# Sliding-window attention on one core: half of one K tile moved from TensorE transposes to VectorE blocks and GpSimd moves, loaded earlier; a 128-column ones tile for the range count

## The chip, the cores and the metric

One core of a Trainium2 chip. The metric is the device time of one execution in microseconds (us); lower is better. Executions over 1.5% slower than the fastest of the same kernel are left out of the means. Medians are quoted. Ratios are the mean time of one kernel's runs over that of the other's in the same rounds, so not quite the ratio of those medians.

Engine names in the profile: PE is TensorE's matmuls, PEld its weight loads, DVE is VectorE, ACT ScalarE, POOL GpSimd, and SP the engine whose queue issues most transfers. The granted clock is the share of the full TensorE clock that the trace records. A pitch is the time from the start of one instruction to the start of the next of its kind. The chain of waits is the chain of work that ended last, followed back from the end of the program.

## The reference

```python
B, Sq, D = 8, 32, 1024;  Hq, Hkv, Dh = 32, 4, 128;  W = 2048      # the last W of 8192 cached rows
q = (x @ wq).reshape(B, Sq, Hq, Dh).transpose(0, 2, 1, 3)
k = repeat(k_cache[:, :, -W:, :], Hq // Hkv);  v = repeat(v_cache[:, :, -W:, :], Hq // Hkv)
p = softmax(einsum("bhqd,bhkd->bhqk", q, k) * Dh ** -0.5)
out = einsum("bhqk,bhkd->bhqd", p, v).transpose(0, 2, 1, 3).reshape(B, Sq, Hq * Dh) @ wo
```

## The kernel before

There are 32 units, one for each batch row and KV head. A unit has four slots. In each slot TensorE makes scores for 512 keys (four matmuls), ScalarE exponentiates them, and TensorE multiplies the slot from two slots ago by V. Query projections, output projections and K transposes are fitted between these as side work. I count slots through the whole program: unit u has slots 4u to 4u+3.

Scores need K transposed. There are three ways to get it, chosen per unit:

- units 0 to 4: TensorE transposes 16 blocks of 128x128, VectorE copies them out of PSUM;
- units 5, 8, 11 and so on: VectorE transposes 32x32 blocks inside each quarter (four instructions), then 16 moves of 32x512 put the quarters in place, 12 on GpSimd and 4 on VectorE in unit 5's case;
- the others: a transposing DMA.

```python
PE_T = (0, 1, 2, 3, 4)
V_T = {5: (2, (5, 6, 8, 10), 10, 17, 12), ...}     # unit: (loaded with unit, slots of blocks, moves from slot, to slot, GpSimd's moves)
...
self.krp = pool("krp", 4)      # K as loaded
self.kbp = pool("kbp", 2)      # K after the block transposes
...
    def kv_pieces(self, ui):
        def blocks(i):
            if i == 0:
                st["kb"] = self.kbp.tile([P, KT, P], BF16, name="kb")
            sl = slice(i * KT // 4, (i + 1) * KT // 4)
            nc.vector.transpose(out=st["kb"][:, sl, :], in_=self.k_raw[ui][:, sl, :])
        def move(k, d):
            ...
            out = self.kT[ui][d * 32:(d + 1) * 32, :, k * 32:(k + 1) * 32]
            in_ = st["kb"][k * 32:(k + 1) * 32, :, d * 32:(d + 1) * 32]
            if d >= V_T[ui][4] // 4:
                nc.vector.tensor_copy(out=out, in_=in_)
            else:
                nc.gpsimd.tensor_scalar(out=out, in0=in_, scalar1=1.0, scalar2=1.0, op0=ALU.mult, op1=ALU.mult)
...
            for c in range(NCH):                                   # one slot
                s_ps = self.ps_s.tile([P, CJ, UQ], FP32, name="s_ps")
                for jj in range(CJ):
                    nc.tensor.matmul(s_ps[:, jj, :], lhsT=self.kT[ui][:, c * CJ + jj, :], rhs=q_u, start=True, stop=True)
                pT = self.ptp.tile([P, CJ, UQ], BF16, name="pT")
                nc.scalar.activation(out=pT[:, :, :], in_=s_ps[:, :, :], func=ACT.Exp, bias=0.0, scale=self.scale)
                ...                                                # P*V of two slots ago
                for k in ((c,) if ui else ...) if nxt else ():
                    nxt[k]()                                       # four TensorE transposes of the next unit's K
                for p in plan[ui * NCH + c]:
                    p()                                            # blocks, moves, projections
```

At the end a matmul with a ones tile of one column counts the softmax sums that lie in range; if one did not, a slower exact path would run.

## Time and profile before

| | before |
|---|---|
| time, median | 186.7 us |
| span of the profiled run | 184.6 us |
| PE busy, share of the span | 98% |
| first scores of unit 5 (slot 20) | 37.41 us |
| GpSimd done with unit 5's K | 37.13 us (28.36 + 8.77) |
| step of the count matmul in the chain | 0.15 us |

The first view is the page of the kernel before: its line of busy times and its line of the chain that ended last.

```profile
PE 180.7 (98%) x2057; PEld 154.0 (83%) x2057; DVE 115.1 (62%) x266; ACT 131.7 (71%) x133; POOL 95.0 (51%) x150
...
PE 93%; DMA 4%; SPq 1%; issue 0%; DVE 0%
```

The kernel is bound by TensorE. Time that another engine takes is free as long as TensorE never waits for it. The windows view shows where that is close. Each line is a stretch of 5 us with the busy time of each engine; the last three columns are the granted clock, the DMA share and the rate.

```profile
core 0: us, PE busy (x) PEld busy (x) DVE busy (x) ACT busy (x) POOL busy (x), PEclk, DMA share, GB/s
25.00:30.00 5.00, 5.00 (x77) 4.81 (x75) 4.87 (x11) 4.63 (x5) 1.52 (x3) 1.00 1.02 399
30.00:35.00 5.00, 5.00 (x68) 4.72 (x66) 4.79 (x11) 4.47 (x5) 4.62 (x7) 1.00 1.17 287
35.00:40.00 5.00, 5.00 (x64) 4.67 (x62) 4.90 (x12) 3.63 (x4) 2.18 (x5) 1.00 1.20 192
40.00:45.00 5.00, 5.00 (x61) 4.63 (x59) 2.97 (x9) 3.53 (x4) 4.62 (x7) 1.00 1.11 372
45.00:50.00 5.00, 5.00 (x63) 4.67 (x62) 2.37 (x8) 3.91 (x4) 4.56 (x8) 1.00 1.13 279
```

The averages of the page (VectorE 62%, GpSimd 51%) say that there is room. This view says that VectorE has none between 25 and 40 us. The timeline of GpSimd alone shows the other engine. Columns: start, time, engine, line, operation, and in brackets the idle time before.

```profile
28.36 8.77 POOL L261 TENSOR_SCALAR kTv<-kb 32x512 bf16<-32x512 bf16 x12 [26.79 <-PE s_ps L468]
39.76 11.78 POOL L261 TENSOR_SCALAR kTv<-kb 32x512 bf16<-32x512 bf16 x16 [2.63 <-PE s_ps L468]
```

GpSimd is idle until 28.36 us and then works through unit 5's 12 moves, 0.73 us each on average. They end at 37.13 us. The timeline of all engines shows when the results are wanted.

```profile
31.30 0.65 DVE L238 COPY kT<-tp 128x1024 bf16<-128x1024 bf16 x1
32.11 0.60 PE L468 MATMUL s_ps<-QT_63,kT 128*128 128x256 bf16 x4
...
35.29 0.71 DVE L251 STREAM_TRANSPOSE kb<-k_raw 128x512 bf16<-128x512 bf16 x1
...
37.41 0.60 PE L468 MATMUL s_ps<-QT_63,kTv 128*128 128x256 bf16 x4
...
39.54 0.65 DVE L410 COPY va_114<-v_sb 128x2048 bf16<-128x2048 bf16 x1
...
40.51 0.62 PE L479 MATMUL o_ps<-va_114,pT 128*128 128x129 bf16 x8
```

Unit 5's scores (37.41) come 0.3 us after GpSimd is done, unit 5's V matmuls (40.51) 0.3 us after VectorE's copy (39.54 + 0.65 = 40.19), and unit 4's first scores (32.11) 0.2 us after the copy that feeds them (31.95). All three are just in time. Last, the chain of waits at the end:

```profile
176.38 0.86 PE op_ps L295 x4
177.25 0.15 PE cnt_ps L533
177.40 4.48 PE op_ps L295 x36
```

### The profile page before, as it was taken

How to read it: one execution, taken by the hardware profiler on the slowest of the kernel's cores; microseconds unless marked ns; L12 is line 12 of the kernel's file. 1: busy time of each engine (PE TensorE's matmuls, PEld its weight loads, DVE VectorE, ACT ScalarE, POOL GpSimd, SP SyncE). 2: the span in 40 equal slices, each digit the busy share in tenths (PEclk: the TensorE clock that was granted, in tenths of full speed). 3: DMA queues.
4: the chain of work that ended last, by engine and by line, in shares of the span. 5: the costliest groups of instructions: out<-in, count | busy, mean ns of one | idle time of the engine just before them, and what ended most of it. 6: DMA issues, size and time to landing. Idle time of an engine off the chain costs nothing.

```text
span 184.6 us, 5057 instructions
## 1 busy us (share of the span) xinstructions
PE 180.7 (98%) x2057; PEld 154.0 (83%) x2057; DVE 115.1 (62%) x266; ACT 131.7 (71%) x133; POOL 95.0 (51%) x150
## 2 busy tenths in 40 slices
PE   8999999999999999999999999999999999999994
PEld 2789999999999999988788899988787888888843
DVE  0119799994586686586468549656754865265363
ACT  2207899787789777787878677887776888888800
POOL 2000007949939959928954990797199379700000
PEclk9999999999999999999999999999999999999999
DMA  5999999999999999999999999999999999993003
GB/s 161 283 390 407 408 396 395 260 182 380 262 355 208 389 250 240 340 321 302 233 396 251 303 378 308 240 249 409 301 301 342 260 275 313 282 269 47 0 30 94
DMA packets 52954, 51.73 MB, mean 280 GB/s; under 512 B 39744, under 2 KB 40256, under 8 KB 52928
## 3 DMA queue, kind: packets, MB, share of 16 engines
q1 hardware_dynamic: 52352, 50.90, 99.0%
q10 hardware_dynamic: 576, 0.49, 0.8%
q8 instruction: 16, 0.26, 0.6%
q14 instruction: 10, 0.08, 0.2%
HBM read 41.42 MB, written 0.52 MB: 227 GB/s over the span
## 4 chain that ended last, share of the span: by engine, by line
PE 93%; DMA 4%; SPq 1%; issue 0%; DVE 0%
PE o_ps L479 31%; PE s_ps L468 30%; PE op_ps L295 15%; PE q_ps L275 11%; DMA wq_sb<-in_wq_dram 4%; PE q_ps L376 2%; PE tp L236 2%; SPq L164 1%; PE kf_ps L369 1%; SPq L320 0%; DVE o_t L305 0%; PE cnt_ps L533 0%
## 5 line engine op out<-in xcount | busy, mean ns | idle before, releaser
L470 ACT ACTIVATE pT<-s_ps 128x1024 bf16<-128x1024 f32 x128 | 128.8, 1025 | 32.5 <-PE s_ps L468 31.5
L261 POOL TENSOR_SCALAR kTv<-kb 32x512 bf16<-32x512 bf16 x140 | 94.1, 672 | 64.9 <-PE s_ps L468 38.3
L479 PEld LDWEIGHTS <-pT 128*128 128x128 bf16 x1024 | 68.5, 98 | 3.1
L468 PEld LDWEIGHTS <-kT 128*128 128x128 bf16 x368 | 34.8, 98 | 10.3
L295 PE MATMUL op_ps<-wo_sb,OT 128*128 128x512 bf16 (+2 forms) x144 | 36.2, 355 | 0.0
L275 PE MATMUL q_ps<-xT,wq_sb 128*128 128x256 bf16 x192 | 28.2, 273 | 0.0
L479 PE MATMUL o_ps<-va_112,pT 128*128 128x129 bf16 x352 | 27.1, 220 | 0.0
L479 PE MATMUL o_ps<-va_113,pT 128*128 128x129 bf16 x352 | 27.0, 220 | 0.0
L479 PE MATMUL o_ps<-va_114,pT 128*128 128x129 bf16 x320 | 24.7, 220 | 0.0
L251 DVE STREAM_TRANSPOSE kb<-k_raw 128x512 bf16<-128x512 bf16 x36 | 23.8, 685 | 1.2 <-DMA k_raw<-in_k_cache_dram 1.2
L416 DVE RECIPROCAL RL_all<-o_ps 128x2 f32<-128x2 f32 x32 | 5.3, 164 | 25.8 <-PE o_ps L479 25.7
L421 DVE TENSOR_SCALAR o_sb<-o_ps,RL_all 128x128 bf16<-128x128 f32 x64 | 19.5, 347 | 1.1
L468 PEld LDWEIGHTS <-kTv 128*128 128x128 bf16 x144 | 13.9, 98 | 5.1
L275 PEld LDWEIGHTS <-wq_sb 128*128 128x128 bf16 x192 | 17.0, 98 | 1.2
L468 PE MATMUL s_ps<-QT_63,kT 128*128 128x256 bf16 x112 | 16.8, 272 | 0.0
L423 DVE STREAM_TRANSPOSE OT<-o_sb 128x256 bf16<-128x256 bf16 x32 | 14.2, 445 | 1.1
L468 PE MATMUL s_ps<-QT_66,kT 128*128 128x256 bf16 x96 | 14.4, 273 | 0.0
L295 PEld LDWEIGHTS <-OT 128*128 128x128 bf16 x144 | 11.4, 98 | 2.3 <-DVE OT L423 0.2
L468 PE MATMUL s_ps<-QT_65,kT 128*128 128x256 bf16 x80 | 12.0, 273 | 0.0
L468 PE MATMUL s_ps<-QT_64,kT 128*128 128x256 bf16 x80 | 12.0, 272 | 0.0
L302 DVE TENSOR_TENSOR oacc<-op_ps,oacc 128x512 f32<-128x512 f32 x8 | 5.5, 682 | 7.4 <-PE op_ps L295 7.4
L410 DVE COPY va_113<-v_sb 128x2048 bf16<-128x2048 bf16 x11 | 9.8, 888 | 0.0
(44 smaller groups left out, 105.6 us busy)
## 6 DMA issues: line engine op xcount, KB each, us to landing
v_sb<-in_v_cache_dram SPq DMA_DIRECT2D x30, 512.0 KB, 7.6
wo_sb<-in_wo_dram SPq DMA_DIRECT2D x16, 512.0 KB, 6.9
wq_sb<-in_wq_dram SPq DMA_DIRECT2D x13, 512.0 KB, 7.5
k_raw<-in_k_cache_dram SPq DMA_DIRECT2D x13, 512.0 KB, 6.4
wq_sb<-in_wq_dram SPq DMA_DIRECT2D x6, 256.0 KB, 6.5
v_sb<-in_v_cache_dram SPq DMA_DIRECT2D x4, 256.0 KB, 4.9
kT<-in_k_cache_dram SPq DMA_TRANSPOSE x36, 7.3
k_raw<-in_k_cache_dram SPq DMA_DIRECT2D x2, 256.0 KB, 7.6
```

The source lines that it names most:

```text
L251: nc.vector.transpose(out=st["kb"][:, sl, :], in_=self.k_raw[ui][:, sl, :])
L261: nc.gpsimd.tensor_scalar(out=out, in0=in_, scalar1=1.0, scalar2=1.0, op0=ALU.mult, op1=ALU.mult)
L275: nc.tensor.matmul(st["ps"][:, 0:self.NQ], lhsT=self.wq_t[g, i][:, c % (DC // 2), hl * P:(hl + 1) * P], rhs=self.xT[:, c, :], start=(c == ...
L295: nc.tensor.matmul(ps[:, 0:w], lhsT=self.OT[:, gq, c, t * P:(t + 1) * P], rhs=self.wo_t[gq][:, c, n0:n0 + w], start=(k == 0), stop=(k == 7))
L302: nc.vector.tensor_tensor(out=acc, in0=ps[:, 0:w], in1=acc, op=ALU.add)
L410: self.nc.vector.tensor_copy(out=self.va[ui % 3][:, :, 0:self.Dh], in_=self.v_sb[ui][:, :, :])
L416: nc.vector.reciprocal(out=rl[:, ui * QT_N:(ui + 1) * QT_N], in_=o_ps[:, :, Dh])
L421: nc.vector.tensor_scalar(out=o_sb[:, qt, :, :], in0=o_ps[:, qt, 0:Dh].rearrange("p (i c) -> p c i", c=4), scalar1=rl[:, ui * QT_N + qt:ui ...
L423: nc.vector.transpose(out=self.OT[:, g * QT_N:(g + 1) * QT_N, :, b * self.Sq:(b + 1) * self.Sq], in_=o_sb[:, :, :, :])
L468: nc.tensor.matmul(s_ps[:, jj, :], lhsT=self.kT[ui][:, c * CJ + jj, :], rhs=q_u, start=True, stop=True)
L470: nc.scalar.activation(out=pT[:, :, :], in_=s_ps[:, :, :], func=ACT.Exp, bias=0.0, scale=self.scale)
L479: nc.tensor.matmul(o_ps[:, qt, 0:self.VW], lhsT=pT[:, jj, qt * P:(qt + 1) * P], rhs=va[:, j, 0:self.VW], start=(j == 0 and qt == 0), stop= ...
```

## The change

It has three parts. The intent is to take eight of unit 4's sixteen transposes off TensorE, the engine that bounds the kernel, and give them to engines that look half idle; to let the count matmul use the whole array width; and to load one late V tile in one transfer.

```diff
-V_HALVES = 30
+V_HALVES = 31
+KH = 4
+KH_SLOTS = ((6, 7), 7, 12)          # slots of the two blocks; moves spread from slot 7 to 12
...
-        self.ones_c = self.c1.tile([P, 1], BF16, name="ones_c")
+        self.ones_c = self.c1.tile([P, P], BF16, name="ones_c")
...
+        if ui == KH - 2:
+            self.load_k(KH, 1)       # second half of K4 right after K2 and V2; the first half stays where it was
...
-        return [lambda i=i: piece(i) for i in range(4)]
+        return [lambda i=i: piece(i) for i in range(2 if ui == KH else 4)]
+
+    def kh_pieces(self):
+        def blocks(i):
+            if i == 0:
+                st["kb"] = self.kbp.tile([P, KT, P], BF16, name="kb")
+            sl = slice(i * H // 2, (i + 1) * H // 2)
+            nc.vector.transpose(out=st["kb"][:, sl, :], in_=self.k_raw[KH][:, H + sl.start:H + sl.stop, :])
+        def move(k, d):
+            nc.gpsimd.tensor_scalar(out=self.kT[KH][d * 32:(d + 1) * 32, H:, k * 32:(k + 1) * 32],
+                                    in0=st["kb"][k * 32:(k + 1) * 32, 0:H, d * 32:(d + 1) * 32],
+                                    scalar1=1.0, scalar2=1.0, op0=ALU.mult, op1=ALU.mult)
...
+        blocks, moves = self.kh_pieces()
+        for k, p in enumerate(blocks):
+            plan[KH_SLOTS[0][k]].append(p)
+        spread(moves, *KH_SLOTS[1:])
...
-        nc.tensor.matmul(cnt[0:1, 0:2 * ncol], lhsT=self.ones_c[:, :], rhs=self.ok[:, :, :], start=True, stop=True)
+        nc.tensor.matmul(cnt[:, 0:2 * ncol], lhsT=self.ones_c[:, :], rhs=self.ok[:, :, :], start=True, stop=True)
```

More of the change, by code (lines that the diff above doesn't have):

```diff
@@ L186, in load_k @@
             H = KT // 2
+            if ui == KH and part == 1:
+                self.k_raw[ui] = self.krp.tile([P, KT, self.Dh], BF16, name="k_raw")
+            if ui == KH and part == 0:
+                nc.sync.dma_start(out=self.k_raw[ui][:, 0:H, :], in_=src.rearrange("(p j) d -> p j d", j=KT)[:, 0:H, :])
+                return
             if part == 1:
@@ L210, in load_unit @@
             if ui not in V_T:
-                self.load_k(ui, None if ui in PE_T else 0)
+                self.load_k(ui, None if ui in PE_T and ui != KH else 0)
             self.load_v(ui, self.nc.sync)
@@ L238, in piece @@
                 nc.vector.tensor_copy(out=self.kT[ui][:, half * 8:(half + 1) * 8, :], in_=st["tp"][:, :, :])
-        return [lambda i=i: piece(i) for i in range(4)]
+        return [lambda i=i: piece(i) for i in range(2 if ui == KH else 4)]
+    def kh_pieces(self):
+        nc, P, KT = self.nc, self.P, self.KT
+        H, st = KT // 2, {}
+        def blocks(i):
[7 more added lines that the diff above has]
+                                    scalar1=1.0, scalar2=1.0, op0=ALU.mult, op1=ALU.mult)
+        return [lambda i=i: blocks(i) for i in range(2)], [lambda k=k, d=d: move(k, d) for k in range(4) for d in range(4)]
     def kv_pieces(self, ui):
@@ L485, in run @@
                     pv_queue.pop(0)()
-                for k in ((c,) if ui else ((), (), (0, 1), (2, 3))[c]) if nxt else ():
+                for k in ((c,)[:len(nxt) - c] if ui else ((), (), (0, 1), (2, 3))[c]) if nxt else ():
                     nxt[k]()
```

## The prediction

> **What bounds it.** TensorE. The page gives PE 98% busy at a full clock, and the chain of waits is 93% PE; the windows table shows PE busy 5.00 of every 5.00 us from 15 us on. Counting four-matmul score groups as "slots" (four per unit), the timeline has score slot 6 at 20.98, 10 at 25.43, 18 at 34.76 and 20 (unit 5, the first fed by GpSimd) at 37.41 us.
>
> **What the change takes off PE.** Eight K4 transposes (and a 0.65 us VectorE copy). Four transposes cost 0.22 us (slots with them are 1.11 us apart, without 0.89): 0.45 us. The count matmul takes 0.15 us in the chain of waits, though its 128 columns should stream in a quarter of a 512-column matmul's 0.215 us. The Trainium skill, "TensorEngine Tiling (Array Packing)", Key Properties, says changing tiling mode drains the array; a 128-wide ones tile should avoid that: at most 0.1 us (this trace shows only the 0.15). V30 in one transfer, the larger memset and the reordered 256 KB load: nothing.
>
> **What it adds.** Two VectorE block transposes (128x512, pitch 0.61 us) and 16 GpSimd moves of 32x256. The 32x512 moves last 0.61 us and repeat every 0.73 us (16 in 11.65 us). A half move is estimated at 0.39 us and, with the same gap, a pitch of 0.4 to 0.5: 6.5 to 8.2 us in all.
>
> **Why that lands on the critical path.** The two engines are full just there.
> - VectorE is busy without a gap from 20.95 to 40 us (4.87, 4.79, 4.90 of 5 us). The new blocks come at slots 6 and 7; the second should end near 25.8 us, so GpSimd starts K4's moves about 25.9 (it idled until 28.36). The copy of V2, ready at 25.2 for a use at 25.86, comes 1.2 us later: a first PE stall of some 0.6 us.
> - Before, the 12 GpSimd moves of unit 5 ran 28.36 to 37.13, only 0.3 us ahead of slot 20. Now 16 half moves join (13 before any of unit 5's): 25.9 + 6.5..8.2 + 8.8 = 41 to 43 us. Slot 20 waits for that.
> - K4's block tile takes the second buffer of its pool, so unit 8's blocks (before: 35.29 us, fresh buffer) now wait until GpSimd has emptied unit 5's; the instruction order shows this new wait. VectorE runs in order: behind it lie unit 3's normalization, query casts and the V5 copy, which ended 4.9 us after that block began. So V5 is ready at about 42 + 5 = 47 us, where its matmuls began at 40.51: about 6.5 us lost.
>
> PE has no idle time later in which to win it back.
>
> **Sum.** 186.7 + 6.7 (GpSimd and VectorE set that end, so the 0.45 us is swallowed) - 0.1 = 193.3 us. Range 190.0 to 195.5. Chances: faster by over 2% 0.02, within 2% 0.13, slower by over 2% 0.85.
>
> **What would show it.** In the timeline: half moves of about 0.39 us, starting near 26; GpSimd without a gap until 41 to 43; unit 5's first score matmul waiting for GpSimd; a VectorE wait of 2 to 5 us before unit 8's first block, released by GpSimd; the first V5 matmul near 46 to 47; PE busy well under 5.00 in the windows from 35 to 50 us, and unchanged pitch after. Count matmul step under 0.1 us.
>
> **What would make it wrong.** Half moves far cheaper than half (at a pitch of 0.2 us unit 5 would be in time, and the result 0.3% faster); GpSimd starting earlier, because VectorE gets to the blocks earlier; or the stalled VectorE catching up, without GpSimd beside it, faster than its 4.9 us.

## The result

193.14 us against 186.69 us (medians of six runs each), ratio 1.0346 with a 95% interval of 1.0288 to 1.0403: slower. Every output was correct.

| | before | after |
|---|---|---|
| time, median | 186.7 us | 193.1 us |
| first scores of unit 5 | 37.41 us | 42.52 us |
| first V matmul of unit 5 | 40.51 us | 47.28 us |
| count matmul step | 0.15 us | 0.06 us |
| mean granted clock, profiled run | 0.999 | 0.989 |

The same two lines of the page, for the changed kernel:

```profile
PE 181.6 (95%) x2033; PEld 154.4 (81%) x2049; DVE 116.3 (61%) x267; ACT 131.6 (69%) x133; POOL 101.4 (53%) x166
...
PE 83%; DVE 6%; DMA 4%; POOL 3%; issue 1%; SPq 1%
```

GpSimd's busy time grew by only 6.4 us and its share by two points, but it and VectorE are now in the chain. The windows show where:

```profile
core 0: us, PE busy (x) PEld busy (x) DVE busy (x) ACT busy (x) POOL busy (x), PEclk, DMA share, GB/s
25.00:30.00 5.00, 4.11 (x57) 3.61 (x55) 4.90 (x11) 3.51 (x4) 3.89 (x9) 1.00 1.04 398
30.00:35.00 5.00, 4.82 (x66) 4.43 (x64) 4.79 (x11) 4.63 (x6) 4.50 (x9) 1.00 1.22 264
35.00:40.00 5.00, 3.54 (x39) 2.78 (x36) 4.11 (x11) 2.58 (x3) 4.48 (x9) 1.00 1.30 186
40.00:45.00 5.00, 2.48 (x23) 2.11 (x24) 1.32 (x2) 1.02 (x1) 4.54 (x8) 0.88 1.12 368
45.00:50.00 5.00, 5.00 (x50) 4.37 (x49) 1.84 (x6) 3.07 (x3) 4.50 (x9) 0.78 1.07 338
```

PE lost 5.05 us of busy time between 25 and 45 us (20 minus 4.11, 4.82, 3.54 and 2.48), and from 45 to 50 us it was busy all the time but at a mean clock of 0.78. Five waits make up the 5.05 us: 0.46, 0.43 and 0.18 us for VectorE's copies, 0.38 us for the last of K4's own half moves, and 3.60 us for unit 5's moves. GpSimd's timeline in the changed kernel:

```profile
25.61 6.63 POOL L262 TENSOR_SCALAR kT<-kb 32x256 bf16<-32x256 bf16 x13 [23.94 <-DVE kb L259]
32.30 2.00 POOL L287 TENSOR_SCALAR kTv<-kb 32x512 bf16<-32x512 bf16 x3
34.36 1.68 POOL L262 TENSOR_SCALAR kT<-kb 32x256 bf16<-32x256 bf16 x3
36.12 9.06 POOL L287 TENSOR_SCALAR kTv<-kb 32x512 bf16<-32x512 bf16 x13
```

K4's half moves repeat every 0.51 us (13 in 6.63). They start at 25.61, when VectorE has finished its second new block, and unit 5's last nine moves cannot begin before 36.12. The chain of waits has the last of them end at 42.48. The timeline of all engines:

```profile
26.15 0.61 PE L509 MATMUL o_ps<-va,pT 128*128 128x129 bf16 x8 [0.46 <-DVE va L436]
...
36.07 0.71 DVE L277 STREAM_TRANSPOSE kb<-k_raw 128x512 bf16<-128x512 bf16 x1 [0.82 <-POOL kT L262]
...
36.09 0.61 PE L498 MATMUL s_ps<-QT,kT 128*128 128x256 bf16 x4 [0.38 <-POOL kT L262]
...
40.33 0.99 DVE L436 COPY va<-v_sb 128x2048 bf16<-128x2048 bf16 x1
...
42.52 0.61 PE L498 MATMUL s_ps<-QT,kTv 128*128 128x256 bf16 x4 [3.60 <-POOL kTv L287]
...
43.90 1.06 PE L498 MATMUL s_ps<-QT,kTv 128*128 128x256 bf16 x4
...
46.47 0.98 PE L498 MATMUL s_ps<-QT,kTv 128*128 128x256 bf16 x4
...
47.28 0.62 PE L509 MATMUL o_ps<-va,pT 128*128 128x129 bf16 x8
```

Read the bracket at 42.52 first: TensorE rested 3.60 us for GpSimd. Then compare score groups of the same size: 0.61 us at 42.52, but 1.06 and 0.98 at 43.90 and 46.47. Those later lines show no wait in brackets; they run slowly. Finally note V5's copy: it was done at 41.32 (40.33 + 0.99), before TensorE went on. At the end of the program:

```profile
183.16 0.86 PE op_ps L321 x4
184.02 0.06 PE cnt_ps L563
184.08 4.43 PE op_ps L321 x36
```

From unit 5's first V matmul on, the two kernels run the same. It came 6.77 us later (47.28 minus 40.51); the spans differ by 6.8 us.

### The profile page after: what moved, and what is told of

Same layout as the page of the kernel before. It is cut to its first block, busy times and chain, and to the rows that moved or that the text cites. A ratio compares the mean times of both kernels' runs of the same rounds, so it can differ in the third digit from the quotient of the medians.

```text
span 191.4 us, 5042 instructions
## 1 busy us (share of the span) xinstructions
PE 181.6 (95%) x2033; PEld 154.4 (81%) x2049; DVE 116.3 (61%) x267; ACT 131.6 (69%) x133; POOL 101.4 (53%) x166
## 4 chain that ended last, share of the span: by engine, by line
PE 83%; DVE 6%; DMA 4%; POOL 3%; issue 1%; SPq 1%
PE o_ps L509 28%; PE s_ps L498 28%; PE op_ps L321 14%; PE q_ps L301 10%; DMA wq_sb<-in_wq_dram 4%; POOL kTv L287 2%; DVE kb L277 2%; PE q_ps L402 2%; DVE o_sb L447 1%; PE tp L245 1%; DVE kT L247 1%; SPq L166 1%; POOL kT L262 1%; DVE OT L449 1%; DVE kb L259 1%
## 5 line engine op out<-in xcount | busy, mean ns | idle before, releaser
L287 POOL TENSOR_SCALAR kTv<-kb 32x512 bf16<-32x512 bf16 x140 | 92.9, 664 | 40.4 <-DVE kb L277 22.9
L509 PE MATMUL o_ps<-va,pT 128*128 128x129 bf16 x1024 | 79.2, 221 | 0.5 <-DVE va L436 0.5
L498 PE MATMUL s_ps<-QT,kT 128*128 128x256 bf16 x368 | 55.2, 273 | 1.1 <-DVE kT L247 0.6
L321 PE MATMUL op_ps<-wo_sb,OT 128*128 128x512 bf16 (+2 forms) x128 | 32.8, 352 | 0.7
L436 DVE COPY va<-v_sb 128x2048 bf16<-128x2048 bf16 x32 | 26.1, 816 | 0.1
L498 PE MATMUL s_ps<-QT,kTv 128*128 128x256 bf16 x144 | 22.4, 280 | 3.6 <-POOL kTv L287 3.6
L262 POOL TENSOR_SCALAR kT<-kb 32x256 bf16<-32x256 bf16 x16 | 7.4, 464 | 24.9 <-DVE kb L259 23.9
L304 DVE CAST QT<-q_ps 128x256 bf16<-128x256 f32 x24 | 9.8, 407 | 14.0 <-PE q_ps L301 14.0
L301 PEld LDWEIGHTS <-wq_sb 128*128 128x128 bf16 x192 | 17.2, 99 | 1.3
L402 PE MATMUL q_ps<-xT,wq_sb 128*128 128x256 bf16 (+1 forms) x80 | 8.0, 253 | 0.2 <-DMA wq_sb<-in_wq_dram 0.2
L402 PEld LDWEIGHTS <-wq_sb 128*128 128x128 bf16 x80 | 6.7, 99 | 1.1 <-DMA wq_sb<-in_wq_dram 0.5
```

The source lines that it names most:

```text
L301: nc.tensor.matmul(st["ps"][:, 0:self.NQ], lhsT=self.wq_t[g, i][:, c % (DC // 2), hl * P:(hl + 1) * P], rhs=self.xT[:, c, :], start=(c == ...
L304: nc.vector.tensor_copy(out=self.q_view(g)[:, :, hl, :], in_=st["ps"][:, 0:self.NQ].rearrange("p (b s) -> p b s", b=self.B))
L321: nc.tensor.matmul(ps[:, 0:w], lhsT=self.OT[:, gq, c, t * P:(t + 1) * P], rhs=self.wo_t[gq][:, c, n0:n0 + w], start=(k == 0), stop=(k == 7))
L402: nc.tensor.matmul(qs[h // 2][:, h % 2, n0:n1], lhsT=self.wq_t[0, c // H][:, c % H, h * P:(h + 1) * P], rhs=self.xT[:, c, n0:n1], start=(c ...
L436: self.nc.vector.tensor_copy(out=self.va[ui % 3][:, :, 0:self.Dh], in_=self.v_sb[ui][:, :, :])
L509: nc.tensor.matmul(o_ps[:, qt, 0:self.VW], lhsT=pT[:, jj, qt * P:(qt + 1) * P], rhs=va[:, j, 0:self.VW], start=(j == 0 and qt == 0), stop= ...
```

## The experiments

The theory was: GpSimd's new work does not fit between the moment its input is there (25.6 us) and unit 5's scores, so a backlog forms and TensorE waits for it; the rest after the wait is a clock that fell. Rivals: the reordered load; VectorE being full; GpSimd slowing VectorE whenever it runs; and, for the slow matmuls, contention instead of the clock. The eleven kernels were run in three calls (a call is one set of rounds; the record names another chip for each), each beside the kernel before, whose medians there were 186.41, 186.53 and 186.57 us.

| run | what differs | us | ratio to before |
|---|---|---|---|
| e2_load_only | changed kernel, K4 whole on TensorE | 186.45 | 1.0006 (0.9976 to 1.0036) |
| e3_blocks | e2 + the two VectorE blocks | 187.55 | 1.0074 (1.0027 to 1.0121) |
| e4_moves_early | e2 + 16 half moves, early source | 187.68 | 1.0084 (1.0048 to 1.0121) |
| e5_moves_late | e2 + 16 half moves, late source | 192.46 | 1.034 (1.0306 to 1.0375) |
| e6_fill | changed kernel + matmuls in the wait | 191.39 | 1.0263 (1.0225 to 1.0301) |
| e1_small_parts | before + ones tile and V30 only | 186.15 | 0.9978 (0.9939 to 1.0016) |
| e7_early | changed kernel, blocks at slots 2, 3 | 186.44 | 1.0015 (0.998 to 1.005) |
| e8_early_share | e7, two more moves on VectorE | 186.88 | 1.0022 (0.9993 to 1.0052) |
| e9_first_half | e7, the other half of K4 | 186.55 | 0.9994 (0.9963 to 1.0024) |
| e11_first_half_share | e9, one more move on VectorE | 186.21 | 0.9991 (0.9965 to 1.0016) |
| e10_three_kb | changed kernel, third block buffer | 193.41 (three runs) | 1.0338 (1.0269 to 1.0407) |

### The load alone

```diff
-        return [lambda i=i: piece(i) for i in range(2 if ui == KH else 4)]
+        return [lambda i=i: piece(i) for i in range(4)]
...
-        for k, p in enumerate(blocks):
-            plan[KH_SLOTS[0][k]].append(p)
-        spread(moves, *KH_SLOTS[1:])
```

> The changed kernel with the early K4 load, the count and the V30 parts, but K4 turned whole on TensorE as before: no VectorE blocks, no GpSimd moves. Backlog theory (GpSimd has more work than fits before unit 5): time as before within 0.5 us, 186.7, unit 5's first scores near 37.4 us, no PE wait. Rival, the reordered 256 KB load delays later loads: a large part of the 6.5 us stays, 190 us or more, with waits released by a DMA.

Measured: 186.45 us, as before. Unit 5's first scores start at 37.69 us and wait for nothing:

```profile
37.69 0.60 PE L494 MATMUL s_ps<-QT,kTv 128*128 128x256 bf16 x4
```

"No PE wait" was not quite met: at 19.68 us TensorE waits 0.48 us for the load of a K tile, but the time does not show it. The load order is not the cause.

### The VectorE blocks alone

The diff of e2, but the loop that plans the blocks stays.

> As e2_load_only, plus the two VectorE blocks at slots 6 and 7, their result unused; K4 turned on TensorE; no moves. Backlog theory: only VectorE is later, by 2 x 0.61 us, less some slack: 0.5 to 1.3 us lost, 187.2 to 188.0, granted clock full. Rival, the full VectorE is the cause by itself: 190 us or more.

Measured: 187.55 us, 1.1 us lost, inside the expected range. Two waits for VectorE appear, the same that the changed kernel has at the same places:

```profile
26.22 0.61 PE L508 MATMUL o_ps<-va,pT 128*128 128x129 bf16 x8 [0.42 <-DVE va L436]
28.60 0.61 PE L497 MATMUL s_ps<-QT,kT 128*128 128x256 bf16 x4 [0.43 <-DVE kT L247]
```

So two blocks at a pitch of 0.61 us cost 1.1 us where VectorE is full. That is a real cost, but a sixth of the loss.

### The moves alone, early and late

```diff
-            nc.gpsimd.tensor_scalar(out=self.kT[KH][d * 32:(d + 1) * 32, H:, k * 32:(k + 1) * 32],
-                                    in0=st["kb"][k * 32:(k + 1) * 32, 0:H, d * 32:(d + 1) * 32],
+            nc.gpsimd.tensor_scalar(out=st["sink"][d * 32:(d + 1) * 32, :, k * 32:(k + 1) * 32],        # read by nobody
+                                    in0=self.k_raw[KH][k * 32:(k + 1) * 32, H:, d * 32:(d + 1) * 32],   # e4
+                                    in0=self.va[2][k * 32:(k + 1) * 32, H:, d * 32:(d + 1) * 32],       # e5
```

Both keep K4 on TensorE and have no blocks, so the outputs stay right. e5's moves are spread from slot 8 instead of 7, after the copy that they read.

> As e2_load_only, plus 16 half moves on GpSimd of the same size, read straight from the loaded K4 half (there near 20 us) into a tile nobody reads; no blocks; K4 turned on TensorE. Backlog theory: 16 x 0.51 = 8.2 us fit into GpSimd's idle time before 28.4, so unit 5 is on time, 186.7 to 187.2. Rival, GpSimd work next to VectorE's copies slows those (the work itself costs, whenever it runs): 188 us or more.

> The same 16 moves as e4_moves_early, but read from the copy of V2, which ends near 25.2 us, so that they start as late as in the changed kernel; no blocks, K4 turned on TensorE. Backlog theory: GpSimd ends unit 5's moves at 25.3 + 8.2 + 8.8 = 42.3 us, the first scores of unit 5 wait until then instead of 37.4: 4.9 us lost, plus 0 to 1.7 us of half clock after the wait: 191.4 to 193.3. If the time were as in e4_moves_early, the start would not matter and the backlog theory falls.

Measured: 187.68 us early, 192.46 us late. The first lines below are of the early run, GpSimd's timeline and then TensorE's:

```profile
21.53 6.29 POOL L264 TENSOR_SCALAR sink<-k_raw 32x256 bf16<-32x256 bf16 x13 [19.86 <-DMA k_raw<-in_k_cache_dram]
...
38.57 0.61 PE L498 MATMUL s_ps<-QT,kTv 128*128 128x256 bf16 x4 [0.82 <-POOL kTv L289]
```

The same for the late run:

```profile
25.23 5.82 POOL L264 TENSOR_SCALAR sink<-va 32x256 bf16<-32x256 bf16 x12 [23.57 <-DVE va L438]
...
41.83 0.95 PE L498 MATMUL s_ps<-QT,kTv 128*128 128x256 bf16 x4 [4.30 <-POOL kTv L289]
```

The early run missed its range (186.7 to 187.2) by half a microsecond. The K4 half was there only at 21.5 us, where I had written 20, and unit 5's moves could not start before 28.38, when TensorE released them, so the moves did not quite fit and TensorE waited 0.82 us for GpSimd. That miss fits the backlog theory and not the rival: the wait is again at unit 5's scores, for GpSimd, and VectorE's copies beside the moves are not slower than in e2_load_only (in both runs 0.65 us for the copy of kT and 0.67 us for that of V2, near 24 us). The same GpSimd work started 3.7 us later (25.23 minus 21.53) delays unit 5's scores by 3.3 us more (41.83 minus 38.57). When the moves start is what costs; that they run at all shows no cost beyond that wait in these traces. e5 alone, without blocks, almost reproduces the loss of the changed kernel.

### TensorE kept busy during the wait

```diff
+N_FILL = 14
...
+                for i in range(N_FILL if ui == 5 and c == 0 else 0):
+                    nc.tensor.matmul(s_ps[:, 0:2, :], lhsT=self.ident[:, :], rhs=self.QT[0][:, 0:512], start=True, stop=True)
                 for jj in range(CJ):
                     nc.tensor.matmul(s_ps[:, jj, :], lhsT=self.kT[ui][:, c * CJ + jj, :], rhs=q_u, start=True, stop=True)
```

> The changed kernel with 14 matmuls of 512 columns (3.0 us at 0.215 us) ahead of unit 5's first scores, written to the score tile that those then overwrite: TensorE works through most of its wait. Clock theory (3.6 us of rest let the granted clock fall to half for 3.4 us, which costs up to 1.7 us): unit 5's first scores still start near 42.5 us, but the clock stays full, three slots from there take 3.1 us instead of 4.0, and the time is 191.0 to 191.8, with granted clock 0.998 or more in every run. Rival, the slow matmuls come from what GpSimd and VectorE do beside them: no change, 193.1.

Measured: 191.39 us, 191.22 to 191.5 in four runs, each with a granted clock of 1.0. TensorE's timeline and then the windows:

```profile
42.42 0.61 PE L501 MATMUL s_ps<-QT,kTv 128*128 128x256 bf16 x4 [0.56 <-POOL kTv L288]
```

```profile
40.00:45.00 5.00, 4.44 (x41) 3.06 (x40) 1.37 (x3) 1.57 (x2) 4.55 (x7) 1.00 1.12 370
45.00:50.00 5.00, 5.00 (x61) 4.63 (x59) 2.72 (x8) 3.54 (x4) 4.56 (x8) 1.00 1.11 268
```

Unit 5's scores start as late as in the changed kernel (42.42 against 42.52), GpSimd works beside them as before (4.55 of 5 us), yet the clock stays at 1.00. From there to the first V matmul of unit 5 (at 45.52) it takes 3.10 us, as in the kernel before, where the changed kernel took 4.76. Useless matmuls made the kernel 1.75 us faster (191.39 against 193.14). The two were not run in the same rounds; each against the kernel before in its own rounds, the losses are 4.86 and 6.45 us. The clock theory holds and contention does not.

The six runs of the changed kernel show the same without an edit: the one with a clock of 1.0 took 191.28 us, those with 0.989 to 0.991 took 193.03 to 193.14 us, those with 0.98 took 193.79 and 193.9 us. The profiled run's clock record has one stretch of half clock, 3.413 us long, besides the last 0.8 us of the span, when TensorE is done. Such a stretch costs 3.413 x 0.5 = 1.7 us and lowers the mean clock over 191.4 us by 0.009; by that estimate 0.991 is one stretch and 0.98 is two. The second stretch then added only about 0.7 us, not 1.7 (193.1 to 193.8 us; 0.6 to 0.75 us in e5 and e10 as well). No trace of a run with two was kept, so why it costs less stays open. The Trainium skill, "TensorE: Matmul & The Clock Gate", Part 1, names the two states and a free-running window of 3413 ns; the trace agrees with the length and with the factor of one half.

### A third buffer for the turned blocks

```diff
-        self.kbp = pool("kbp", 2)
+        self.kbp = pool("kbp", 3)
```

> The changed kernel with a third buffer for the turned blocks, so unit 8's first block on VectorE waits for no GpSimd move. The prediction's last step (that wait makes V5 late) would have 1.5 us or more come back: 191.5 or less. What the trace of the changed kernel shows (the wait was 0.8 us and V5 was ready 1.2 us before TensorE went on): the wait goes, the time stays, 192.5 to 193.5, or 191.3 in a run without half clock.

Measured: 193.41 us, the median of the three runs 193.41, 191.48 (clock 1.0) and 194.16; a fourth, 194.45, is left out here and in the ratio (with it the median is 193.79, just over the expected range). VectorE's block for unit 8 now waits for nothing:

```profile
35.75 0.71 DVE L277 STREAM_TRANSPOSE kb<-k_raw 128x512 bf16<-128x512 bf16 x1
```

The wait went and the time stayed. So this wait was not part of the loss, against the prediction. (Run by run: 191.48 against 191.28 us at clock 1.0, 193.41 against 193.03 to 193.14 at about 0.99.)

### The small parts alone

The kernel before with the three edits of `V_HALVES`, `ones_c` and `cnt` from the diff above.

> The kernel before with only the 128-column ones tile and V30 in one transfer. 186.5 to 186.8, not to be told from before; in the chain of waits the count matmul takes 0.06 us instead of 0.15.

Measured: 186.15 us, 0.35 us below the expected range; ratio 0.9978 with an interval that holds 1, so not to be told from before. The chain of waits:

```profile
177.14 0.06 PE cnt_ps L533
```

The 0.09 us are visible in the trace, in this run and in every other with the wide tile, but not in the time. The transfer of V30 was not run by itself.

### Earlier blocks, and who does the moves

e7 loads the K4 half ahead of K2 and plans the blocks where VectorE still has gaps. e8 is e7 with two more of unit 5's moves on VectorE. The comments mark which run each line belongs to.

```diff
-KH_SLOTS = ((6, 7), 7, 12)
+KH_SLOTS = ((2, 3), 3, 9)
...
+        self.load_k(KH, 1)                       # the early load; the one after V2 is removed
         for ui in range(2, 4):
             self.load_unit(ui)
...
-            if d >= V_T[ui][4] // 4:
+            if d >= V_T[ui][4] // 4 or (ui == 5 and d == 2 and k >= 2):      # e8 only
```

> The changed kernel with K4's half loaded ahead of K2 and its blocks at slots 2 and 3, where VectorE had some 1.2 us to spare. Backlog theory: GpSimd starts near 20.5, has done K4's half by 28.7 and unit 5 by about 37.5, against a need at 37.0: 186.5 to 187.3, no half clock. If VectorE's or the loads' lack of time were the cause, it would stay above 189.

> As e7_early, with two more of unit 5's moves on VectorE instead of GpSimd (10 and 6), so GpSimd ends near 36.0 us, ahead of the need: the 0.45 us of transposes and 0.09 us of the count come through: 186.0 to 186.5, 0.3% faster than before.

Measured: 186.44 us, 0.06 us below its range (186.5 to 187.3), and 186.88 us. e7's GpSimd timeline and two lines of its TensorE timeline (unit 4's and unit 5's first scores):

```profile
20.43 7.99 POOL L260 TENSOR_SCALAR kT<-kb 32x256 bf16<-32x256 bf16 x16 [18.77 <-DVE kb L257]
28.52 8.78 POOL L285 TENSOR_SCALAR kTv<-kb 32x512 bf16<-32x512 bf16 x12
```

```profile
32.18 0.61 PE L497 MATMUL s_ps<-QT,kT 128*128 128x256 bf16 x4 [0.18 <-DVE kT L245]
...
37.50 0.60 PE L497 MATMUL s_ps<-QT,kTv 128*128 128x256 bf16 x4
```

The same work, started five microseconds sooner, costs nothing: all of the 6.5 us came back, with the transposes off TensorE. This is the strongest evidence for the backlog. But e7 is no faster than before. Unit 4's first scores, which in the kernel before came 0.2 us after VectorE's copy, now wait for it. Their slot lasts 1.23 us instead of 0.89, so 0.34 of the 0.45 us saved are lost there. e8 missed its range (186.0 to 186.5): the two extra moves made VectorE late for V5, and TensorE waited 0.34 us for that copy:

```profile
41.19 0.61 PE L508 MATMUL o_ps<-va,pT 128*128 128x129 bf16 x8 [0.34 <-DVE va L435]
```

### The other half of K4

e9 is e7 with the halves exchanged: blocks and moves turn rows 0 to 7, TensorE rows 8 to 15, so that VectorE's copy is wanted two slots later. e11 adds one more move of unit 5 on VectorE.

```diff
-            half, q = i // 2, i % 2
+            half, q = i // 2 + (ui == KH), i % 2
...
-            nc.vector.transpose(out=st["kb"][:, sl, :], in_=self.k_raw[KH][:, H + sl.start:H + sl.stop, :])
+            nc.vector.transpose(out=st["kb"][:, sl, :], in_=self.k_raw[KH][:, sl, :])
...
-            nc.gpsimd.tensor_scalar(out=self.kT[KH][d * 32:(d + 1) * 32, H:, k * 32:(k + 1) * 32],
+            nc.gpsimd.tensor_scalar(out=self.kT[KH][d * 32:(d + 1) * 32, 0:H, k * 32:(k + 1) * 32],
...
-            if d >= V_T[ui][4] // 4:
+            if d >= V_T[ui][4] // 4 or (ui == 5 and d == 2 and k == 3):      # e11 only
```

> As e7_early, but the blocks and moves turn the first half of K4 and TensorE turns the second, whose VectorE copy is wanted two slots later. In e7_early unit 4's first scores waited 0.18 us for the VectorE copy of the first half, which gave most of the saved 0.45 us back. If that copy is where the gain went: unit 5's first scores start 0.1 to 0.2 us sooner counted from slot 5 (then held by GpSimd, which ends near 37.3): 186.2 to 186.5. If not: as e7_early.

> As e9_first_half, with one more of unit 5's moves on VectorE (11 on GpSimd), so GpSimd ends near 36.6 us and no longer holds unit 5: 0.3 to 0.5 us faster than before by the trace's slots, 186.0 to 186.3. If VectorE is too full for it, as in e8_early_share, a wait for the V5 copy appears and it is no faster than before.

Measured: 186.55 us, just above its range (186.2 to 186.5), and 186.21 us; neither can be told from before (intervals 0.9963 to 1.0024 and 0.9965 to 1.0016). Counted from slot 5 to slot 20, e9 takes 17.38 us where e7 took 17.52, as expected. The trace of e11 shows the gain arriving and partly leaving. From slot 5 to slot 20 it takes 17.12 us (20.02 to 37.14) against 17.55 us in the kernel before (19.86 to 37.41): 0.43 of the 0.45 us. Then slot 22 lasts 1.48 us instead of 1.33: V5's copy ends at 40.33, and the matmuls that read it could have started at 40.23. What remains is too small for these rounds. No version that is clearly faster than the kernel before was found.

## Why the prediction was right, and where it was not

- **The time, right:** 193.3 predicted, 193.14 measured, in the range 190.0 to 195.5.
- **GpSimd's backlog, right in place and size:** start "about 25.9", measured 25.61; end 41 to 43, measured 42.48; unit 5's scores waiting for it, shown. e4, e5 and e7 confirm that the start decides. A half move took 0.40 us (median) as estimated (0.39; the prediction does not say how that was worked out); its mean pitch, 0.51 us, was just over the 0.4 to 0.5 assumed, because three of the sixteen took 0.74 to 0.75 us. Why these three took longer, no run shows.
- **The first stall, right:** "some 0.6 us", measured 0.46. A second of 0.43 us, for VectorE's copy of a K tile, and two of 0.18 and 0.38 us before unit 5 were not foreseen. e3 shows that the blocks alone cost 1.1 us in all.
- **The swallowed gain, right:** the 0.45 us of transposes did not appear, since another engine set the pace. Even with the backlog gone (e7) VectorE's copy took most of it back.
- **The count, right:** 0.06 us instead of 0.15. The Trainium skill's sentence in "TensorEngine Tiling (Array Packing)", Key Properties, that a change of tiling mode drains the array, fits; no run separates a drain from another effect of the narrow tile.
- **The last step, wrong:** the prediction said that unit 8's blocks "now wait until GpSimd has emptied unit 5's", that VectorE would stand 2 to 5 us, and V5 would be ready at about 47 us. The wait was 0.82 us. It ended when the last K4 move was done, with nine of unit 5's moves still to come, so the buffer that unit 8 took was K4's. V5's copy was ready at 41.32, and e10 shows that the wait cost nothing. The instruction order had shown that VectorE waits for GpSimd, but not for which of its moves; I assumed the worse one.
- **What took its place:** the half clock. The prediction expected an "unchanged pitch after" the wait. Of the 6.77 us by which unit 5's first V matmul was late, 5.11 (42.52 minus 37.41) are the delay of its scores, and the remaining 1.66 are two slots and the scores of a third, run largely at half clock. e6 shows both: with the rest filled, the scores are just as late and the 1.75 us are gone. The backlog alone gives 5.1 of the 6.7 us predicted. That the sum came out right to 0.2 us was luck: the wrong last step (about 1.9 us: V5 at 47 instead of 42 plus the 3.1 us that the kernel before takes from unit 5's scores to its V matmuls) and the missing half clock (1.66 us) were of nearly equal size.

## What to carry to other kernels

An engine that is idle half the time on average has no room where its input arrives late and its output is wanted soon: compare when the new work can start and when the next result is due, at that place. Work taken off the bounding engine is only gained if every engine that feeds it was ahead by that much; here three hand-overs had 0.2 to 0.3 us of slack. And a rest of TensorE can have a second price (3.6 us here, then up to 1.7 us more at half clock), so when one cannot be avoided, try to fill it with matmuls.

## What the Trainium skill lacked or had wrong

- "TensorE: Matmul & The Clock Gate", the table of "Why this matters for your kernels", says that one window of idle brings back half clock. In the profiled run of the changed kernel TensorE was idle about 3.6 us, but the half clock began at 43.8 us, 1.3 us after it had started again (42.52). Counting windows of 3.413 us back from there, the last one (40.4 to 43.8) had only about 2.1 us of rest in it; in e10 and e5 it had 2.8 and 3.3 us. So in this case a window need not be idle throughout.
- The same page calls the window free-running, but says only for the start of a kernel what follows from that. Three profiled runs (the changed kernel, e5, e10) all have the half clock beginning 37.547 us after the first full grant, 11 times 3.413, although their waits began 32.7, 33.1 and 33.4 us after it. The half clock at the end of the program also begins a whole number of windows after the first full grant (54 in the changed kernel, 52 in the kernel before). Whether one rest costs no, one or two such stretches differs from run to run: 191.28, 193.1 and 193.8 us for the same kernel.
- "GPSIMD Engine Reference", Part 3, gives rates per element, but no fixed cost of an instruction with one input. Here a 32x512 bf16 move took 0.61 us and a 32x256 one 0.40 us (medians), so by a straight line through the two some 0.19 us of each do not depend on the size (an estimate). Back to back they repeat every 0.73 and 0.51 us on average, as some moves take about 0.35 us longer.
- "TensorEngine Tiling (Array Packing)", Key Properties, gives no size for the drain at a change of mode. One 128x1 matmul between two full-width ones took 0.15 us of the chain, a 128x128 one 0.06 us.
